# Layer B head loop of a four-layer spectral / recurrent-memory kernel: fixed issue order on three engines, column sums in one block, and PSUM banks shared out anew

## The chip, the cores and the metric

The kernel runs on one core of one Trainium2 chip. The metric is device time in microseconds (us) of the whole launch, lower is better. TensorE is called PE below, VectorE DVE, ScalarE ACT, GpSimd POOL, the DMA-issuing engine SP.

## The reference

Two kinds of layer alternate, A, B, A, B, each after a layer norm and with a residual. The change touches layer B only:

```python
# layer B: S = 2048 tokens of 640 in 64 segments of 32; 8 memory rows; 32 heads of 128
for s in range(n_seg):
    h = concat([mem, xs], axis=1)                      # 40 rows
    q, k, v = h @ Wq, h @ Wk, h @ Wv                   # per head
    p = softmax(where(mask, q @ k.T * Dh**-0.5, -1e9))
    o = (p @ v) @ Wo
    mem = o[:, :M]                                     # goes into the next segment
    outs.append(o[:, M:])
```

The kernel guesses all memories at once, computes all 64 segments in parallel, and checks the guess at the end (a slow path, not taken with these inputs, repeats what fails). So layer B is 32 heads in one long loop, followed by the output projection.

## The kernel before

Work of one head on PE: five Q chains and five K chains (each five accumulating matmuls of up to 502 columns), four or five V tiles, nine score parts (19 matmuls), five value groups (19 matmuls), and the softmax sums: 19 matmuls with a stationary matrix of ones, 128 rows by 32 columns, that write four 32-partition strips of PSUM and so use four column tiles of the array. The heads are staggered: iteration `h` projects head `h`, scores head `h-1` and forms values of head `h-2`. A scheduler decides the final order on each engine.

PSUM has eight banks and before the change all are taken: 2 for projections (`pj`), 2 for scores, 2 for values, 2 for the sums tile `psl`, of whose second bank only 139 columns in one strip are used.

```python
pj = octx.enter_context(tc.tile_pool(name="b_pj", bufs=2, space=PSUM))
pa = octx.enter_context(tc.tile_pool(name="b_pa", bufs=2, space=PSUM))
# ...
def q_run(w, h, g_):
    ps = pj.tile([128, 512], FP32, name="psq", tag="pj")
    chain(w["Wq"], h % 2, ps[:, 0:hi - lo], hT, lo, hi)                    # 5 matmuls
    nc.scalar.mul(out=qv[:, :, 0:SEG], in_=x_view(ps, o, n)[:, :, 1:SW], mul=scale)     # 480 columns
    if g_ < NG - 1:
        nc.vector.tensor_scalar_mul(out=qv[:, :, SEG], in0=..., scalar1=scale)          # 15 columns
    # ... two more small scalings on nc.vector, two on nc.scalar
def k_run(w, h, g_):      # psk in pj, 5 matmuls, one nc.vector copy to KT
def v_tiles(w, hp, t):    # psv in pj, 10 matmuls, one nc.scalar copy to V
def score_part(h, P, part):
    ps = pa.tile([128, 512], FP32, name="pss", tag="pss")
    # ... matmuls K'Q ...
    nc.scalar.activation(out=E[:, 0:n], in_=ps[:, 0:n], func=ACTF.Exp)
    nc.vector.tensor_tensor(out=P[:, o0:o0 + n], in0=E[:, 0:n], in1=bs.mask[:, o0:o0 + n], op=ALU.mult)
def sums(h, P):
    psl = pa.tile([128, 2, 512], FP32, name="psl", tag="psl", bufs=1)
    # ... 19 matmuls with ones32 into psl ...
    nc.scalar.copy(out=sums_sb[:, 0:GQ], in_=psl[:, 0, 0:GQ])
    nc.scalar.copy(out=sums_sb[0:32, GQ:GQ + NL], in_=psl[0:32, 1, 0:NL])
    nc.scalar.activation(out=R[:], in_=sums_sb[:], func=ACTF.Ln, ...)
    nc.scalar.activation(out=R[:], in_=R[:], func=ACTF.Exp, scale=-1.0)    # R = 1 / sums
    # ... R to DRAM, then broadcast to 128 partitions as Rb (1 MB) ...
    nc.gpsimd.tensor_tensor(out=accR[:], in0=accR[:], in1=R[:], op=ALU.add)          # range check
    nc.gpsimd.tensor_tensor(out=accS[:], in0=accS[:], in1=sums_sb[:], op=ALU.add)
# value_group: pso in pa (2 banks); DVE multiplies pso by Rb into oT, oTm
```

## Time and profile before

1843.58 us, median of 3 runs (1839.65 to 1844.62).

Part 1 of the page: busy time of each engine, its share of the span, and instructions.

```profile
span 1841.2 us, 36901 instructions
PE 1709.3 (93%) x14778; PEld 1149.3 (62%) x14779; DVE 938.2 (51%) x2792; ACT 793.7 (43%) x1874; POOL 222.5 (12%) x180
```

A window of the first head loop: its stretch, length, busy time of each engine, granted clock, DMA share and rate.

```profile
core 0: us, PE busy (x) PEld busy (x) DVE busy (x) ACT busy (x) POOL busy (x), PEclk, DMA share, GB/s
303.30:748.00 444.70, 428.28 (x3731) 281.42 (x3727) 253.03 (x776) 245.44 (x611) 76.61 (x50) 1.00 0.36 126
```

PE is busy 96% of the loop and nothing else comes near. "Busy", however, covers matmuls that wait inside their modelled end, so the loop has to be read from the starts of matmuls too. Two heads take 35.5 us (the last sums matmuls of three even heads end at 375.46, 410.96 and 446.46 us). Dividing the start-to-start intervals of PE in four quiet heads (374.9 to 445.95 us) gives, per head, 15.65 us of streaming at N columns / 2.4 + 2.5 ns, 1.08 us around the sums, 0.91 us of waits and 0.11 us of small rest. The Trainium skill, "TensorE: Matmul & The Clock Gate", Back-to-back issue gap, gives that pitch for isolated matmuls on a warm clock, and other figures for a stream in which every matmul has a weight load (about 131 ns at 512 columns, 81 ns at 128). The trace has such a stream (14779 weight loads for 14778 matmuls) and follows the first: the starts are 209 ns apart at 495 columns, 109 ns at 256 and 55 ns at 128.

The waits view of PE: who waited for whom, total us, times, longest.

```profile
PE psq L678 <- DVE QT_2047 L721: 13.7, 15, 1.0
PE psq L678 <- DVE QT_25002 L721: 13.7, 15, 1.0
PE pso L787 <- DVE oTmf L793: 6.9, 11, 1.1
```

The first two lines, one a layer, are Q chains waiting for a projection bank until DVE has done the 15-column scaling. The third is value groups waiting for a value bank, which DVE frees only after it has multiplied by `Rb`: these are the waits for a late broadcast of R, meant by "late broadcast" below. The timelines of PE, DVE and POOL around one such wait (start, duration, engine, line, operation; idle time and its releaser in brackets):

```profile
502.46 1.22 PE L678 MATMUL psq<-hTf,wWq 128*128 128x495 bf16 x5
503.52 0.29 PE L751 MATMUL pss<-QT_2046,KT_2048 128*128 128x132 bf16 x2
504.76 1.21 PE L678 MATMUL psq<-hTf,wWq 128*128 128x499 bf16 x5 [0.96 <-DVE QT_2047 L721]
...
506.33 0.40 PE L787 MATMUL pso<-P,V 128*128 128x132 bf16 x4
506.65 0.23 PE L767 MATMUL psl<-P,ones_72 128*32 128x132 bf16 x1
506.91 0.27 PE L751 MATMUL pss<-QT_2046,KT_2048 128*128 128x141 bf16 x2
507.11 0.23 PE L767 MATMUL psl<-P,ones_72 128*32 128x132 bf16 x1
```

```profile
503.07 1.50 DVE L755 TENSOR_TENSOR P<-E,maskf 128x283 bf16<-128x283 bf16 x1 [0.68 <-ACT E L754]
504.50 0.21 DVE L721 TENSOR_SCALAR QT_2047<-psq 128x15 bf16<-128x15 f32 x1
```

```profile
502.88 1.53 POOL L778 TENSOR_TENSOR accR<-accR,R 128x634 f32<-128x634 f32 x1 [0.45 <-ACT R L772]
```

The mask multiply takes 1.50 us while POOL adds `accR`, the small scaling stands behind it in DVE's queue, and PE stands still for 0.96 us. The PE lines also show the sums (`psl`, tile 128*32) as single matmuls strewn between others; a head has three sums blocks on average.

### The profile page before, as it was taken

The page shows a single profiled execution, that of the slowest core. Times are in us where ns is not written, and L with a number is a line of the kernel's source. Part 1 is how long each engine was busy: PE and PEld are TensorE (multiplying, and loading weights), DVE is VectorE, ACT ScalarE, POOL GpSimd, SP SyncE. Part 2 cuts the span into 40 slices and gives each one's busy share as a digit, 9 for nine tenths or more (in the row PEclk, how much of TensorE's full clock was granted, in tenths as well). Part 3 has the DMA queues.
Part 4 walks back from the last instruction along what each step waited for, and adds up shares of the span by engine and source line. Part 5 has one row for each costly group of instructions (what it writes and reads, how often), then busy time and mean ns, then how long its engine had stood idle before and what let it go on. Part 6 is the DMA issues. An engine that isn't in the chain of part 4 may idle for free. (4 is left out here: it accounts for less than half of the span.)

```text
span 1841.2 us, 36901 instructions
## 1 busy us (share of the span) xinstructions
PE 1709.3 (93%) x14778; PEld 1149.3 (62%) x14779; DVE 938.2 (51%) x2792; ACT 793.7 (43%) x1874; POOL 222.5 (12%) x180
## 2 busy tenths in 40 slices
PE   4987999999999999999959879999999999999998
PEld 2655656666666666677736556666666666666776
DVE  5557255556555555543345562555556555555111
ACT  4334354555555555400023444555555555554000
POOL 0100011111112112100000000111111111111000
PEclk9999999999999999999979989999999999999999
DMA  5764033343343332374164530333433333333630
GB/s 138 190 216 136 16 123 107 121 140 131 104 142 133 118 135 98 129 234 146 51 156 89 217 113 23 117 117 131 146 116 126 128 128 118 134 121 108 208 129 31
DMA packets 148012, 233.10 MB, mean 127 GB/s; under 512 B 8480, under 2 KB 119664, under 8 KB 138096
## 3 DMA queue, kind: packets, MB, share of 16 engines
q1 hardware_dynamic: 141632, 203.72, 32.5%
q0 software_dynamic: 6192, 26.86, 5.8%
q8 instruction: 120, 1.97, 0.4%
q14 instruction: 68, 0.56, 0.1%
HBM read 191.30 MB, written 50.35 MB: 131 GB/s over the span
## 5 line engine op out<-in xcount | busy, mean ns | idle before, releaser
L678 PE MATMUL psq<-hTf,wWq 128*128 128x128 bf16 (+3 forms) x1560 | 310.2, 336 | 36.0 <-DVE QT_2047 L721 13.7
L741 PE MATMUL psv<-wWv,hTf 128*128 128x256 bf16 x2720 | 330.3, 272 | 1.6 <-DVE KT_2048 L734 0.2
L754 ACT ACTIVATE E<-pss 128x269 bf16<-128x269 f32 (+5 forms) x576 | 210.7, 383 | 253.6 <-PE pss L751 240.4
L678 PE MATMUL psk<-hTf,wWk 128*128 128x495 bf16 (+3 forms) x1600 | 317.2, 342 | 0.5 <-DVE hTf L961 0.3
L741 PEld LDWEIGHTS <-hTf 128*128 128x128 bf16 x2720 | 258.0, 97 | 31.4 <-issue 1.7
L755 DVE TENSOR_TENSOR P<-E,maskf 128x269 bf16<-128x269 bf16 (+5 forms) x576 | 221.2, 389 | 65.0 <-ACT E L754 49.7
L743 ACT CAST V<-psv 128x512 bf16<-128x512 f32 (+1 forms) x288 | 162.0, 563 | 207.7 <-PE psv L741 207.7
L678 PEld LDWEIGHTS <-wWq 128*128 128x128 bf16 x1580 | 129.6, 97 | 157.1 <-issue 43.6
L779 POOL TENSOR_TENSOR accS<-accS,sums_sb 128x634 f32<-128x634 f32 x64 | 98.2, 1534 | 998.5 <-ACT sums_sb L770 998.5
L678 PEld LDWEIGHTS <-wWk 128*128 128x128 bf16 x1600 | 136.2, 97 | 113.8 <-issue 1.4
L502 PE MATMUL psx<-Wo_sb,oTxl 128*128 128x320 bf16 x1440 | 203.4, 299 | 0.0
L502 PEld LDWEIGHTS <-oTxl 128*128 128x128 bf16 x1440 | 140.9, 98 | 54.7
L787 PE MATMUL pso<-P,V 128*128 128x132 bf16 (+8 forms) x1216 | 128.5, 216 | 6.9 <-DVE oTmf L793 6.9
L516 DVE TENSOR_TENSOR xo<-psx,xr 128x320 bf16<-128x320 f32 x64 | 31.3, 490 | 175.2 <-PE psx L502 175.2
L791 DVE TENSOR_TENSOR oT<-pso,Rb 128x480 bf16<-128x480 f32 (+1 forms) x160 | 92.9, 581 | 53.3 <-PE pso L787 39.9
L787 PEld LDWEIGHTS <-V 128*128 128x128 bf16 x1216 | 92.7, 98 | 14.5 <-issue 8.2
L778 POOL TENSOR_TENSOR accR<-accR,R 128x634 f32<-128x634 f32 x64 | 97.9, 1529 | 27.4 <-ACT R L772 25.9
L199 PEld LDWEIGHTS <-YT 128*128 128x128 bf16 x640 | 63.1, 99 | 27.1 <-DVE wi L76 2.2
L249 PE MATMUL psg<-GT,UT 128*128 128x320 bf16 x384 | 67.3, 312 | 1.8 <-ACT UT L222 1.8
L89 ACT ACTIVATE lnnb<-lnmv,eps 128x2 f32<-128x2 f32 (+2 forms) x36 | 10.7, 300 | 133.6 <-DVE lnmv L82 132.9
L250 ACT CAST G<-psg 128x640 bf16<-128x640 f32 x64 | 44.3, 692 | 52.4 <-PE psg L249 49.6
L791 DVE TENSOR_TENSOR oT<-pso,oT_2044 128x480 bf16<-128x480 f32 (+1 forms) x80 | 46.5, 581 | 37.1 <-PE pso L787 29.0
(646 smaller groups left out, 2194.6 us busy)
## 6 DMA issues: line engine op xcount, KB each, us to landing
Rb<-Rd SPq DMA_DIRECT2D x32, 1059.5 KB
oTx_d<-oT SPq DMA_DIRECT2D x60, 512.0 KB
oTxl<-oTx_d SPq DMA_DIRECT2D x18, 1024.0 KB
oT_2044<-Rd SPq DMA_DIRECT2D x16, 1059.5 KB
oT_24999<-Rd SPq DMA_DIRECT2D x16, 1059.5 KB
Wv_sb<-in_B_Wv_dram POOLq DMA_DIRECT2D x10, 1024.0 KB, 9.5
wWq<-in_B_Wq_dram SPq DMA_DIRECT2D x32, 320.0 KB
wWk<-in_B_Wk_dram SPq DMA_DIRECT2D x32, 320.0 KB
```

The source lines that it names most:

```text
L199: nc.tensor.matmul(ps[:, cout, 0:NF], lhsT=lhsT, rhs=Fd[:, ch, FD_IDX[(cin, cout)], :], start=(n == 0), stop=(n == 9))
L249: nc.tensor.matmul(psg[:, i, 0:320], lhsT=lhsT, rhs=Gd[:, ch, i * 320:(i + 1) * 320], start=(ch == 0), stop=(ch == 2))
L502: self.tc.nc.tensor.matmul(ps[:, 0:320], lhsT=lhs(h, k // 2 % 4), rhs=self.g["Wo_sb"][:, h, c0:c0 + 320], start=(h == 0), stop=(h == H - 1))
L678: nc.tensor.matmul(ps, lhsT=w[:, ch, hh * 128:(hh + 1) * 128], rhs=src[:, ch, lo:hi], start=(ch == 0), stop=(ch == 4))
L741: nc.tensor.matmul(ps[:, i * 256:(i + 1) * 256], lhsT=hT[:, ch, (t + i) * 128:(t + i + 1) * 128], rhs=w["Wv"][:, ch, :], start=(ch == 0), ...
L743: nc.scalar.copy(out=V[:, t:t + n, :].rearrange("p a b -> p (a b)"), in_=ps[:, 0:n * 256])
L754: nc.scalar.activation(out=E[:, 0:n], in_=ps[:, 0:n], func=ACTF.Exp)
L755: nc.vector.tensor_tensor(out=P[:, o0:o0 + n], in0=E[:, 0:n], in1=bs.mask[:, o0:o0 + n], op=ALU.mult)
L778: nc.gpsimd.tensor_tensor(out=accR[:], in0=accR[:], in1=R[:], op=ALU.add)
L779: nc.gpsimd.tensor_tensor(out=accS[:], in0=accS[:], in1=sums_sb[:], op=ALU.add)
L787: nc.tensor.matmul(pso[:, lo - q0:hi - q0], lhsT=V[:, t, (h % 2) * 128:(h % 2 + 1) * 128], rhs=P[:, off:off + hi - lo], start=(i == 0), st ...
L791: nc.vector.tensor_tensor(out=oT[:, s0 * SEG:(s0 + ns) * SEG].rearrange("p (s t) -> p s t", t=SEG), in0=po[:, :, 0:SEG], in1=pr[:, :, 0:SE ...
```

## The change

Intent: keep PE fed by fixing the issue order of the head loop on PE, ACT and DVE by hand; run the column-tiled sums as one block; put the fifth sums strip into the unused end of the last score bank, so that `psl` needs one bank and projections get three; let ACT alone release a Q bank.

```diff
-    pj = octx.enter_context(tc.tile_pool(name="b_pj", bufs=2, space=PSUM))
+    pj = octx.enter_context(tc.tile_pool(name="b_pj", bufs=3, space=PSUM))
 # q_run, and likewise two more small scalings
-                nc.vector.tensor_scalar_mul(out=qv[:, :, SEG], in0=x_view(ps, o, n)[:, :, 0], scalar1=scale)
+                nc.scalar.mul(out=qv[:, :, SEG], in_=x_view(ps, o, n)[:, :, 0], mul=scale)
 # sums
-            psl = pa.tile([128, 2, 512], FP32, name="psl", tag="psl", bufs=1)
+            psl = pa.tile([128, 512], FP32, name="psl", tag="psl", bufs=1)
+            ps4 = ps_last[0:32, 512 - NL:512]              # end of the last score part's bank
-                    nc.tensor.matmul(psl[32 * j:32 * j + 32, b, ...
+                    dst = psl[32 * g_:32 * g_ + 32, :] if g_ < 4 else ps4
+                    nc.tensor.matmul(dst[:, ...
 # head loop
+        with tc.manual_schedule(engines={nc.tensor.engine, nc.scalar.engine, nc.vector.engine}):
+            for h in range(H + 2):
 # ... dense = Q, K, V pieces; parts = scores; groups = values, interleaved as before ...
+                if h < H:
+                    merge(dense, parts + groups)
+                if 1 <= h <= H:
+                    Rb[h - 1] = sums(h - 1, P[h - 1], last_ps[h - 1])
 # ... the last two iterations and the check's banks rearranged ...
```

The bank count stays at eight: 3 projections, 2 scores, 2 values, 1 sums.

More of the change, by code (lines that the diff above doesn't have):

```diff
@@ L720, in q_run @@
             if g_ < NG - 1:
-                nc.vector.tensor_scalar_mul(out=qv[:, :, SEG], in0=x_view(ps, o, n)[:, :, 0], scalar1=scale)
+                nc.scalar.mul(out=qv[:, :, SEG], in_=x_view(ps, o, n)[:, :, 0], mul=scale)
             if g_ == 0:
-                nc.vector.tensor_scalar_mul(out=QT[:, QPRE:NQ], in0=ps[:, 0:PRE], scalar1=scale)
+                nc.scalar.mul(out=QT[:, QPRE:NQ], in_=ps[:, 0:PRE], mul=scale)
             elif g_ == NG - 2:
@@ L726, in q_run @@
             elif g_ == NG - 1:
-                nc.vector.tensor_scalar_mul(out=x_view(QT, st.qbase(NSEG - 4), 4)[:, :, SEG], in0=ps[:, 0:3 * SW + 1:SW], scalar1=scale)
+                nc.scalar.mul(out=x_view(QT, st.qbase(NSEG - 4), 4)[:, :, SEG], in_=ps[:, 0:3 * SW + 1:SW], mul=scale)
                 q_tail(QT, ps, 0, 3 * SW + 1, SEG - st.TAIL)
@@ L755, in score_part, with sums @@
             nc.vector.tensor_tensor(out=P[:, o0:o0 + n], in0=E[:, 0:n], in1=bs.mask[:, o0:o0 + n], op=ALU.mult)
+            return ps
         runs = [[(t, r) for t in range(NT) for r in st.tiles[t] if r[0] == g_] for g_ in range(NG)]
-        def sums(h, P):
-            psl = pa.tile([128, 2, 512], FP32, name="psl", tag="psl", bufs=1)
+        def sums(h, P, ps_last):
+            psl = pa.tile([128, 512], FP32, name="psl", tag="psl", bufs=1)
+            ps4 = ps_last[0:32, 512 - NL:512]
             for i in range(max(len(r) for r in runs)):
@@ L765, in sums @@
                     t, (_, lo, hi, off) = runs[g_][i]
-                    b, j = divmod(g_, 4)
-                    nc.tensor.matmul(psl[32 * j:32 * j + 32, b, lo - st.q0[g_]:hi - st.q0[g_]], lhsT=ones32[:], rhs=P[:, off:off + hi - lo],
+                    dst = psl[32 * g_:32 * g_ + 32, :] if g_ < 4 else ps4
+                    nc.tensor.matmul(dst[:, lo - st.q0[g_]:hi - st.q0[g_]], lhsT=ones32[:], rhs=P[:, off:off + hi - lo],
                                      start=(i == 0), stop=(i == len(runs[g_]) - 1), skip_group_check=True)
-            nc.scalar.copy(out=sums_sb[:, 0:GQ], in_=psl[:, 0, 0:GQ])
-            nc.scalar.copy(out=sums_sb[0:32, GQ:GQ + NL], in_=psl[0:32, 1, 0:NL])
+            nc.scalar.copy(out=sums_sb[:, 0:GQ], in_=psl[:, 0:GQ])
+            nc.scalar.copy(out=sums_sb[0:32, GQ:GQ + NL], in_=ps4)
             nc.scalar.activation(out=R[:], in_=sums_sb[:], func=ACTF.Ln, bias=g["floor"][:, 0:1])
@@ L815, in begin @@
         def begin():
-            ps = psx()
-            first.append(ps)
-            out.accumulate(ps, len(first) - 1, lambda h, j: oT0[:, h, j * 128:(j + 1) * 128], 0, HPRE)
+            k = len(first)
+            first.append(psx())
+            return [lambda a=a: out.accumulate(first[k], k, lambda h, j: oT0[:, h, j * 128:(j + 1) * 128], a, a + 4) for a in range(0, HPRE, 4)]
         def merge(dense, dep):
@@ L827, in merge @@
                     n += 1
-        P, Rb, oT, w = {}, {}, {}, None
-        for h in range(H + 2):
-            dense, dep = [], []
-            if h < H:
-                if h % 2 == 0:
+        P, Rb, oT, last_ps, w = {}, {}, {}, {}, None
+        with tc.manual_schedule(engines={nc.tensor.engine, nc.scalar.engine, nc.vector.engine}):
+            for h in range(H + 2):
+                if h < H and h % 2 == 0:
                     w = load_w(h // 2)
@@ L842, in _b_fast_pass @@
                     guess[1](pj, vb)
-                if h < 2:
-                    dense.append(lambda: q_m(w, h))
-                else:
-                    dense += [lambda g_=g_: q_run(w, h, g_) for g_ in range(NG)]
-                dense += [lambda g_=g_: k_run(w, h, g_) for g_ in range(NG)]
-                vt = [lambda t=t: v_tiles(w, h // 2, t) for t in range(0, NT, 2)]
-                dense += vt[5:] if h % 2 else vt[:5]
-            else:
-                dense += [begin] * (1 if h == H else 2)
@@ L852, in _b_fast_pass @@
-            if 1 <= h <= H:
-                P[h - 1] = sm.tile([128, st.NP], BF16, name="P", tag="P")
-                dep += [lambda part=part: score_part(h - 1, P[h - 1], part) for part in st.parts]
-            if h >= 2:
-                oT[h - 2] = oTs.tile([128, st.NX], BF16, name="oT", tag="oT")
-                dep += [lambda g_=g_: value_group(h - 2, P[h - 2], Rb[h - 2], oT[h - 2], g_) for g_ in range(NG)]
-            merge(dense, dep)
-            if 1 <= h <= H:
-                Rb[h - 1] = sums(h - 1, P[h - 1])
@@ L861, in _b_fast_pass @@
-            if h >= 2:
-                store(h - 2, oT[h - 2])
+                dense, parts, groups = [], [], []
+                if h < H:
+                    if h < 2:
+                        dense.append(lambda: q_m(w, h))
+                    else:
+                        dense += [lambda g_=g_: q_run(w, h, g_) for g_ in range(NG)]
+                    dense += [lambda g_=g_: k_run(w, h, g_) for g_ in range(NG)]
+                    vt = [lambda t=t: v_tiles(w, h // 2, t) for t in range(0, NT, 2)]
+                    dense += vt[5:] if h % 2 else vt[:5]
@@ new lines, in _b_fast_pass @@
+                if 1 <= h <= H:
+                    P[h - 1] = sm.tile([128, st.NP], BF16, name="P", tag="P")
+                    parts = [lambda part=part: last_ps.update({h - 1: score_part(h - 1, P[h - 1], part)}) for part in st.parts]
+                if h >= 2:
+                    oT[h - 2] = oTs.tile([128, st.NX], BF16, name="oT", tag="oT")
+                    groups = [lambda g_=g_: value_group(h - 2, P[h - 2], Rb[h - 2], oT[h - 2], g_) for g_ in range(NG)]
+                if h < H:
+                    merge(dense, parts + groups)
@@ L864, in _b_fast_pass @@
+                if h == H:
+                    merge(begin(), parts)
+                if 1 <= h <= H:
+                    Rb[h - 1] = sums(h - 1, P[h - 1], last_ps[h - 1])
+                if h == H:
+                    merge(begin(), groups)
+                if h > H:
+                    merge(begin(), [])
+                    merge([lambda: None], groups)
+                if h >= 2:
+                    store(h - 2, oT[h - 2])
     with octx:
@@ L866, in _b_fast_pass @@
         op = octx.enter_context(tc.tile_pool(name="b2_o", bufs=2))
-        psl = pa.tile([128, 2, 512], FP32, name="psl", tag="psl", bufs=1)
-        _b_mem_check(tc, g, pj, [psl[:, 0, :], psl[:, 1, :]], wk, oTm, None,
+        pc = [pa.tile([128, 512], FP32, name="pc0", tag="psl", bufs=1), pa.tile([128, 512], FP32, name="pc1", tag="pso")]
+        _b_mem_check(tc, g, pj, pc, wk, oTm, None,
                      lambda c: [(PRE, st.NC, gq[:, c, 1:NSEG]), (0, PRE, gq[:, c, 1:2].to_broadcast([128, PRE]))], st.NM, st.NC, flag_col,
@@ L885, in psx @@
             n[0] += 1
-            if n[0] % 2:
+            if n[0] % 3:
                 return pj.tile([128, 512], FP32, name="psx", tag="pj")
```

## The prediction

> **What bounds it now.** TensorE. The page of the profile gives PE busy 1709.3 of 1841.2 us (93%), VectorE 51%, ScalarE 43%; the two head loops (220 to 770, 1130 to 1690 us) are 60% of the span. In steady state two heads take 35.5 us there (last sums matmul at 410.86 and 446.36 us in the PE timeline), 17.75 us a head. There PE is 96% busy at granted clock 1.00.
>
> What those 17.75 us hold, from start-to-start intervals of the matmuls in the trace: Q and K chains 8.97 us, V 4.64, scores and values about 1.05 each: 15.7 us of plain streaming. The other 2 us are:
> - Sums. The 128x32 matmuls run 4 to 20 ns apart inside a block, but entering a block delays about 92 ns and leaving it costs 150 to 267 ns. A head has three blocks on average (13 and 6; 12, 5, 1 and 1), about 1.1 us in all. The Trainium skill, "TensorEngine Tiling (Array Packing)", Key Properties, says that changing the tiling mode drains TensorE; the trace agrees.
> - The fourth Q chain waits for a projection bank: the waits view puts 27.4 us, 30 waits, on psq after the VectorE scaling of QT, about 0.96 us every second head. That scaling queues behind a mask multiply that takes 1.50 us instead of 0.3 while GpSimd adds accR. ("GPSIMD Engine Reference", Key points: GpSimd shares SBUF interfaces with VectorE; the trace agrees.) Smaller waits add about 0.3 us a head.
>
> **What the change does.**
> - One sums block per head instead of three: estimate 0.09 + 0.3 + 0.16, so about 0.55 us instead of 1.1. Gain 0.5 us a head.
> - Q banks released by ScalarE alone, three banks instead of two. The small scalings should cost ScalarE about 0.1 us each in its stream (the existing 4- and 28-column ones start the next instruction so soon). Gain about 0.8 us a head.
> - New waits: ScalarE must now finish the four sums instructions (R ready about 2.5 us after the sums) before the first Q scaling. Walking the queue by these durations, third and fifth score part wait for their exponentials: I estimate 0.3 us a head lost.
> - Values stand later as a row (after all scores), so the broadcast of R may bind: the third group needs it about 9.3 us after R is ready. Before, even heads were served by 8.7 and seldom waited; odd heads had the broadcast issued late (4.6 us after R, behind a weight load), and the changed order issues it before that load. I allow 8 us in total for late broadcasts.
> - Tail and output phase stay.
>
> Head: 17.75 to about 16.75 us, 60 heads: 60 us; edge heads 4; minus 8 for late broadcasts. Nearly all is on the critical path: PE is the chain.
>
> **Predicted: 1788 us, range 1770 to 1815.** Faster by over 2%: 0.85, within 2%: 0.14, slower: 0.01.
>
> **What would show it.** Sums: one block of 19 per head, under 0.65 us. Waits view: psq after VectorE QT gone; psq or pss after ScalarE small, under 0.4 us a head. Waits of pso on oTmf still under 15 us. Two heads in 33 to 34 us. PE busy in the loops near 98%. Layer A and output stretches unchanged within 3 us.
>
> **What would make it wrong.** The broadcast of R landing later than 9.3 us in many heads (then about 1815); ScalarE's fixed order holding Q banks longer than walked; small scalings costing 0.2 us each.

## The result, and the profile after

1766.47 us, median of 4 runs (1764.23 to 1768.78). Ratio to before 0.9587, 95% interval 0.9569 to 0.9606: 4.1% faster. The result lies 3.5 us below the predicted range.

Part 1 of the page after, and the window of its first loop:

```profile
span 1762.3 us, 36912 instructions
PE 1664.0 (94%) x14778; PEld 1136.0 (64%) x14779; DVE 863.2 (49%) x2432; ACT 816.8 (46%) x2234; POOL 222.9 (13%) x180
```

```profile
296.00:691.20 395.20, 394.45 (x3581) 265.34 (x3583) 211.96 (x598) 245.38 (x732) 73.66 (x48) 1.00 0.40 136
```

PE is now busy 99.8% of that window. The page's groups of value matmuls, before (first fence) and after (second); the last part of each line is the idle time of PE just before them and its releaser:

```profile
L787 PE MATMUL pso<-P,V 128*128 128x132 bf16 (+8 forms) x1216 | 128.5, 216 | 6.9 <-DVE oTmf L793 6.9
```

```profile
L789 PE MATMUL pso<-P,V 128*128 128x132 bf16 (+8 forms) x1216 | 120.1, 216 | 2.6 <-DVE oTmf L795 2.5
```

The waits that a late broadcast of R causes did not grow but fell, from 6.9 to 2.5 us in these two profiles. The timeline of PE after, from the end of one head to the Q chains of the next:

```profile
492.60 0.27 PE L789 MATMUL pso<-P,V 128*128 128x7 bf16 x3
492.80 0.24 PE L769 MATMUL psl<-P,ones 128*32 128x132 bf16 x4
492.87 0.17 PE L769 MATMUL pss<-P,ones 128*32 128x7 bf16 x1
...
493.26 1.23 PE L678 MATMUL psq<-hTf,wWq 128*128 128x502 bf16 x5
494.33 0.31 PE L751 MATMUL pss<-QT,KT 128*128 128x132 bf16 x3
494.48 1.21 PE L678 MATMUL psq<-hTf,wWq 128*128 128x495 bf16 x5
495.52 0.28 PE L751 MATMUL pss<-QT,KT 128*128 128x148 bf16 x2
495.64 1.21 PE L678 MATMUL psq<-hTf,wWq 128*128 128x495 bf16 x5
496.79 0.28 PE L751 MATMUL pss<-QT,KT 128*128 128x132 bf16 x2
496.91 1.22 PE L678 MATMUL psq<-hTf,wWq 128*128 128x499 bf16 x5
```

All 19 sums matmuls go by between 492.80 and 493.26, and the fourth Q chain (496.91) starts 0.12 us after the score part before it. The timeline of ACT over the same time:

```profile
495.11 0.73 ACT L774 ACTIVATE R<-R 128x634 f32<-128x634 f32 x1
495.75 0.55 ACT L719 ACTIVATE QT<-psq 128x480 bf16<-128x480 f32 x1
496.20 0.23 ACT L721 ACTIVATE QT<-psq 128x15 bf16<-128x15 f32 x1
496.26 0.18 ACT L723 ACTIVATE QT<-psq 128x7 bf16<-128x7 f32 x1
496.32 0.42 ACT L754 ACTIVATE E<-pss 128x283 bf16<-128x283 f32 x1
```

ACT reaches the first Q scaling only at 495.75, 2.5 us after that head's sums, when the third Q chain has already begun in a third bank. With two banks that chain would have needed the first chain's bank, which is read until 496.44.

The same division of PE's starts as before, in four quiet heads (378.6 to 444.5 us), us per head:

| | before | after | prediction took |
|---|---|---|---|
| streaming | 15.65 | 15.65 | 15.7 |
| sums: entering, inside, leaving | 1.08 | 0.55 | 1.1 to 0.55 |
| waits: Q chains before, score parts after | 0.91 | 0.19 | 0.8 to 0.3 |
| small rest | 0.11 | 0.07 | not counted |
| head | 17.75 | 16.46 | 17.75 to 16.75 |

Over 28 heads of each layer the sums' ends advance 499.63 and 498.40 us before, 462.06 and 463.76 us after: 72.2 of the 78.9 us between the two profiled spans. The rest lies outside these heads.

### The profile page after: what moved, and what is told of

Its sections match the earlier page's. It is cut to its first block, busy times and chain, and to the rows that moved or that the text cites. A ratio compares the mean times of both kernels' runs of the same rounds, so it can differ in the third digit from the quotient of the medians.

```text
span 1762.3 us, 36912 instructions
## 1 busy us (share of the span) xinstructions
PE 1664.0 (94%) x14778; PEld 1136.0 (64%) x14779; DVE 863.2 (49%) x2432; ACT 816.8 (46%) x2234; POOL 222.9 (13%) x180
## 5 line engine op out<-in xcount | busy, mean ns | idle before, releaser
L755 DVE TENSOR_TENSOR P<-E,maskf 128x269 bf16<-128x269 bf16 (+5 forms) x576 | 199.6, 355 | 350.1 <-ACT E L754 350.1
L741 PE MATMUL psv<-wWv,hTf 128*128 128x256 bf16 x2720 | 340.4, 272 | 0.0
L754 ACT ACTIVATE E<-pss 128x269 bf16<-128x269 f32 (+5 forms) x576 | 246.3, 429 | 152.0 <-PE pss L751 144.3
L734 DVE CAST KT<-psk 128x495 bf16<-128x495 f32 (+3 forms) x320 | 191.2, 598 | 41.9 <-PE psk L678 41.8
L751 PEld LDWEIGHTS <-KT 128*128 128x128 bf16 x1216 | 113.6, 98 | 116.4 <-issue 16.3
L719 ACT ACTIVATE QT<-psq 128x480 bf16<-128x480 f32 x300 | 170.0, 567 | 0.0
L751 PE MATMUL pss<-QT,KT 128*128 128x132 bf16 (+8 forms) x1216 | 159.5, 216 | 2.7 <-ACT E L754 2.6
L793 DVE TENSOR_TENSOR oT<-pso,oT 128x480 bf16<-128x480 f32 (+1 forms) x160 | 93.2, 583 | 60.3 <-PE pso L789 49.7
L199 PE MATMUL ps<-Fd,YT 128*128 128x321 bf16 x640 | 104.4, 306 | 4.4 <-DMA Fd<-cFd 2.8
L502 PE MATMUL psx<-Wo_sb,oT 128*128 128x320 bf16 x608 | 98.7, 302 | 4.1 <-DVE oT L793 4.1
```

Source lines behind the costliest of these rows:

```text
L199: nc.tensor.matmul(ps[:, cout, 0:NF], lhsT=lhsT, rhs=Fd[:, ch, FD_IDX[(cin, cout)], :], start=(n == 0), stop=(n == 9))
L502: self.tc.nc.tensor.matmul(ps[:, 0:320], lhsT=lhs(h, k // 2 % 4), rhs=self.g["Wo_sb"][:, h, c0:c0 + 320], start=(h == 0), stop=(h == H - 1))
L734: nc.vector.tensor_copy(out=KTs[h % 2][:, lo:hi], in_=ps[:, 0:hi - lo])
L741: nc.tensor.matmul(ps[:, i * 256:(i + 1) * 256], lhsT=hT[:, ch, (t + i) * 128:(t + i + 1) * 128], rhs=w["Wv"][:, ch, :], start=(ch == 0), ...
L751: nc.tensor.matmul(ps[:, off - o0:off - o0 + hi - lo], lhsT=KT[:, t * 128:(t + 1) * 128], rhs=QT[:, lo:hi], start=True, stop=True)
L793: nc.vector.tensor_tensor(out=oT[:, s0 * SEG:(s0 + ns) * SEG].rearrange("p (s t) -> p s t", t=SEG), in0=po[:, :, 0:SEG], in1=pr[:, :, 0:SE ...
```

## The experiments

Each ran three timed rounds against the kernel before, and each gave a correct result. "Per head" is the advance of the sums' ends over 24 heads of the first layer; the ledgers are those of the table, over the same 24 heads, so that they hold occasional waits for late broadcasts too (before: 17.89 us a head, waits 1.06; after: 16.49 us, waits 0.23). A run with another number of projection banks also shares the tiles of the output phase (`psx`) out over the banks accordingly; the diffs leave that line out.

### Scalings on ACT alone

```diff
 # kernel before, q_run: three small scalings
-  nc.vector.tensor_scalar_mul(...)
+  nc.scalar.mul(...)
```

> Kernel before, with only the small Q scalings moved from VectorE to ScalarE. Theory A (the Q chain waits because the VectorE scaling queues behind a slow mask multiply): the waits of psq on VectorE QT, 27 us in total before, vanish and most of the 0.9 us of waits a head goes, so 1800 to 1812 us. Theory B (two banks or the scheduled order hold PE, whoever does the scaling): the wait only changes its name to ScalarE, and the time stays within 8 us of 1843. The sums blocks stay at about three a head in both.

Measured 1849.11 us, ratio 1.0045 (1.0023 to 1.0067): slightly slower, within 2%. Theory A fails here. The 27.4 us of Q waits on DVE are gone; a smaller Q wait on ACT and other waits stand in their place, as the waits view of PE shows:

```profile
PE psv L741 <- DVE KT L734: 13.5, 16, 1.9
PE psq L678 <- ACT QT L723: 11.9, 58, 0.5
PE pss L751 <- ACT E L754: 10.6, 28, 0.4
```

The ledger has 0.89 us of waits a head and 1.35 us for the sums, which the scheduler now puts into 3.5 blocks. Taking DVE out of the release of a bank brought nothing here, with two banks; since the scheduler also rearranged the sums, this run does not show what the move does with the order held.

### No additions on POOL

```diff
-            nc.gpsimd.tensor_tensor(out=accR[:], in0=accR[:], in1=R[:], op=ALU.add)
-            nc.gpsimd.tensor_tensor(out=accS[:], in0=accS[:], in1=sums_sb[:], op=ALU.add)
```

> Kernel before without the two GpSimd additions per head (they only feed a range check, which then always passes; the output stays right). If the slow mask multiply is made by GpSimd on the shared memory interface, the 283-column multiply falls from a mean of 862 ns to about 300, the psq waits on VectorE QT fall from 27 us to under 5, and the time falls by 20 to 35 us. If the multiply is slow for another reason, or the wait has another cause, neither moves: within 8 us of 1843.

Measured 1807.49 us, ratio 0.9819 (0.9797 to 0.9840): 34 us less. The group of the 283-column mask multiply, before and in this run (busy us, mean ns, idle before):

```profile
L755 DVE TENSOR_TENSOR P<-E,maskf 128x283 bf16<-128x283 bf16 x64 | 55.2, 862 | 20.2 <-ACT E L754 20.2
```

```profile
L755 DVE TENSOR_TENSOR P<-E,maskf 128x283 bf16<-128x283 bf16 x64 | 19.5, 305 | 20.1 <-ACT E L754 20.1
```

The waits of `psq` on DVE's scaling, 27.4 us before, no longer stand in this run's waits view, and PE runs its matmuls of the loop in the same order as before. So the prediction's origin of the wait is shown: POOL's additions stretch the mask multiply and with it the wait for the Q bank. The Trainium skill says in "GPSIMD Engine Reference", Key points, that POOL shares its SBUF interfaces with VectorE and contends with two-input instructions; 862 against 305 ns agrees. In the trace before, all 60 mask multiplies of over 0.6 us overlap an addition on POOL and end 0.15 to 0.17 us after it. But this kernel cannot drop the additions, which feed the range check. This is a diagnosis, not a version.

### The fixed order alone

```diff
 # changed kernel, with
-  pj bufs=3, psl one bank, small scalings on nc.scalar
+  pj bufs=2, psl two banks, small scalings on nc.vector
```

> The fixed order alone, with its one sums block per head, but two projection banks, a two-bank sums tile, and the Q scalings on VectorE as before. Theory A: the sums blocks give 0.54 us a head (32 us), but ScalarE now finishes the four sums instructions before the first Q scaling, so with two banks the third Q chain waits about 0.9 us in every head, and the wait behind the mask multiply stays: 1835 to 1875 us. Theory B (the fixed order is what brings the gain): under 1790.

Measured 1886.28 us, ratio 1.0239 (1.0220 to 1.0258): 45 us slower than before. The sums are in one block (0.55 us a head), yet a head takes 18.45 us. The waits view of PE:

```profile
PE psq L678 <- ACT E L754: 50.1, 60, 0.8
PE psk L678 <- ACT QT L685: 36.8, 60, 0.6
PE psv L741 <- DVE KT L734: 12.7, 63, 0.5
```

The ledger has 2.19 us of waits a head. Fixing this order with two banks stalls Q, K and V chains in every head: ACT comes to the Q banks only after the four sums instructions, and PE, in strict order, has nothing to fill in.

### The changed kernel under the scheduler

```diff
-        with tc.manual_schedule(engines={nc.tensor.engine, nc.scalar.engine, nc.vector.engine}):
+        with ExitStack():
```

> The changed kernel with the three engines' fixed order taken off: the scheduler decides again; three banks and scalings on ScalarE stay. If the gains add: the Q waits stay gone (about 0.7 us a head) and the sums lie in about three blocks again (0.54 us a head lost): 1795 to 1810. If the order makes the whole gain: above 1825. If the order is worth nothing: within 8 us of 1766.

Measured 1764.23 us, ratio 0.9578 (0.9560 to 0.9596), against 0.9587 of the changed kernel: the same. The expected 1795 to 1810 was a miss. In the loop the scheduler itself puts the 19 sums matmuls into one block a head; over 24 heads its order of PE's 3588 matmuls is the fixed one. So the fixed order is worth nothing here, and the single block does not come from it.

### Scalings back on DVE

```diff
 # changed kernel, q_run: three small scalings
-  nc.scalar.mul(...)
+  nc.vector.tensor_scalar_mul(...)
```

> The changed kernel with the small Q scalings back on VectorE; order and three banks stay. Theory A (the move to ScalarE removes the wait): the fourth and fifth Q chain wait again behind the mask multiply, 1790 to 1810. Theory B (the third bank hides it): walking the queues, the slow multiply ends about 0.3 us before the bank is needed, so within 8 us of 1766.

Measured 1759.05 us, ratio 0.9555 (0.9534 to 0.9576): within the band of theory B, and 7 us below the changed kernel by the medians, though the intervals overlap. In the ledger the score waits of 0.19 us a head are gone and 0.05 us of waits remain. So in the fixed order that wait is made by the small scalings in ACT's queue. Whether the move costs time is not shown: under the scheduler the kernel with three banks is no faster with them on DVE (1767.67 us, "The third bank alone") than on ACT (1764.23 us, the run above).

### Two projection banks

```diff
-    pj = octx.enter_context(tc.tile_pool(name="b_pj", bufs=3, space=PSUM))
+    pj = octx.enter_context(tc.tile_pool(name="b_pj", bufs=2, space=PSUM))
```

> The changed kernel with two projection banks; order and ScalarE scalings stay. ScalarE starts the first Q scaling 2.4 us after the sums, so the third Q chain, due 2.4 us after the sums, waits until about 3.2: 0.8 us a head, 1805 to 1825. If the third bank is not needed once the scalings are on ScalarE: within 8 us of 1766.

Measured 1853.07 us, ratio 1.0057 (1.0040 to 1.0073): the whole gain is lost, 87 us, more than expected, although PE's order in the loop is that of the changed kernel. The waits view of the first loop (285 to 715 us, 24 heads):

```profile
PE psq L678 <- ACT QT L723: 16.6, 24, 0.7
PE psk L678 <- ACT QT L685: 6.9, 24, 0.3
PE psv L741 <- DVE KT L734: 4.2, 22, 0.2
```

The expected wait of the third Q chain is there, 0.69 us on average in this view and 0.86 us by starts; the first K chain (0.46) and the first V tile (0.36) also wait, which the expectation had not counted.

### Three sums blocks, first try

```diff
+   step = [lambda i=i: sum_steps(h - 1, P[h - 1], last_ps[h - 1], i, i + 1) for i in range(2)]
+   groups = groups[:2] + step[:1] + groups[2:4] + step[1:] + groups[4:]
    merge(dense, parts + groups)
```

> The changed kernel with the 19 sums matmuls of a head in three blocks (two pieces of five and four go between value groups), nothing else moved. If entering and leaving a block is the cost: two more blocks of about 0.09 plus 0.15 us a head, 60 heads: 25 to 35 us slower than 1766. If the cost is the matmuls themselves: within 8 us of 1766.

Measured 1841.65 us, ratio 0.9993 (0.9977 to 1.0010): 75 us slower than the changed kernel, far over the expectation. The experiment was not clean. Two more pieces in the merge list shifted the interleaving, so that two score parts followed the first Q chain and the third part came too early. Its timeline of PE:

```profile
498.69 0.38 PE L678 MATMUL psq<-hTf,wWq 128*128 128x502 bf16 x1
498.90 0.43 PE L751 MATMUL pss<-QT,KT 128*128 128x132 bf16 x5
499.16 1.21 PE L678 MATMUL psq<-hTf,wWq 128*128 128x495 bf16 x5
501.37 0.28 PE L751 MATMUL pss<-QT,KT 128*128 128x132 bf16 x2 [1.00 <-ACT E L754]
```

Of the loss, 0.36 us a head (0.91 against 0.55) lies around the sums; 1.16 us is this new wait. What follows about blocks is nothing yet; about fixed orders, that one score part moved forward can cost a microsecond in every head.

### Three sums blocks in place

```diff
-   groups = groups[:2] + step[:1] + groups[2:4] + step[1:] + groups[4:]
+   groups[1] = lambda a=groups[1], b=step[0]: (a(), b())
+   groups[3] = lambda a=groups[3], b=step[1]: (a(), b())
```

> The changed kernel with the sums in three blocks, each early piece now tied to the value group ahead of it, so that no score part moves. If a block's entering and leaving is the cost: 0.36 us a head by the trace of the first try, 22 us, so 1784 to 1794 us, and no wait of a score part over 0.3 us. If it is free: within 8 us of 1766. If the 75 us of the first try were all due to the blocks: above 1825.

Measured 1790.52 us, ratio 0.9706 (0.9688 to 0.9724): 24 us slower than the changed kernel. The sums take 0.91 us a head instead of 0.55, and the score waits 0.25 us instead of 0.19. So a further block costs 0.18 us, and two of them in 60 heads an estimated 22 us (60 x 0.36); the profiled run, 30 us slower, had more late broadcasts too. The Trainium skill, "TensorEngine Tiling (Array Packing)", Key Properties, says that changing the tiling mode drains TensorE. The trace agrees with a cost at each change, and its size is now known for this loop.

### The third bank alone

```diff
 # kernel before, scheduler order, scalings on nc.vector
-    pj ... bufs=2
+    pj ... bufs=3
-            psl = pa.tile([128, 2, 512], ...)
+            psl = pa.tile([128, 512], ...)
+            ps4 = ps_last[0:32, 512 - NL:512]
```

> The kernel before with the third projection bank and the one-bank sums tile that frees it, nothing else: the scheduler orders, VectorE scales. Theory now: the third bank takes the Q wait out of PE's way and, because the scheduler then sees no gap to fill, leaves the sums in one block. So it makes the whole gain: 1752 to 1768 us, at or below the changed kernel, PE waits under 0.25 us a head. Rival: fixed order or ScalarE scalings have a part of their own: 1785 or more.

Measured 1767.67 us, ratio 0.9590 (0.9574 to 0.9606): the whole gain, with no fixed order and no scaling moved. Its PE order in the steady loop is that of the changed kernel, sums block included. The Q wait on DVE, 27.4 us before, has shrunk to this line of the waits view:

```profile
PE psq L678 <- DVE QT L721: 0.4, 2, 0.2
```

The ledger has 0.55 us for the sums and 0.42 us of waits a head, of which 0.20 are late broadcasts (five in 24 heads of this run); without them the waits are 0.22, of which, by starts, 0.14 are Q chains and 0.08 score parts.

### The one-bank sums tile alone

```diff
 # as the last one, but
-    pj ... bufs=3
+    pj ... bufs=2
```

> As the run with the third bank alone, but with two projection banks: the one-bank sums tile by itself. If the bank makes the gain, the Q wait is back (about 0.9 us a head) and the built order shows two sums blocks a head (one saved, 0.28 us): 1820 to 1848 us. If the tile itself were the gain: under 1790.

Measured 1834.32 us, ratio 0.9953 (0.9936 to 0.9969). The Q wait is back in the waits view of PE:

```profile
PE psq L678 <- DVE QT L721: 29.2, 31, 1.0
```

There are two sums blocks a head (0.78 us). Between this run and the one before, 67 us, lies only the third bank. By the two ledgers it takes 0.80 us a head off the waits (1.22 to 0.42) and 0.23 us off the sums, which the scheduler then puts into one block.

### The sums block early, fixed order

```diff
                 if h < H:
+                    if groups:
+                        groups.insert(1, lambda: Rb.update({h - 1: sums(h - 1, P[h - 1], last_ps[h - 1])}))
                     merge(dense, parts + groups)
-                if 1 <= h <= H:
+                if h == 1 or h == H:
                     Rb[h - 1] = sums(h - 1, P[h - 1], last_ps[h - 1])
```

> The changed kernel with the sums block one value group after the last score part, before most V tiles, instead of at the head's end. ScalarE then does the sums instructions in the V phase and the broadcast of R has 5 us more. Expected: the two score waits (0.19 us a head, 11 us) and the late-broadcast waits (about 4 us in all) go: 1748 to 1758 us. Rival: the four sums instructions hold up the V evictions on ScalarE, PE waits for V banks instead: 1762 to 1785.

Measured 1739.41 us, ratio 0.9444 (0.9429 to 0.9460): 27 us below the changed kernel, more than expected. It is the best version here. The window of its first loop:

```profile
273.00:663.00 390.00, 390.00 (x3570) 264.36 (x3569) 200.97 (x599) 249.97 (x732) 73.67 (x48) 1.00 0.45 139
```

PE is never idle. The ledger has no wait over 40 ns in 24 heads, late broadcasts included, and both layers take 16.27 us a head. The early place also moves POOL's additions away from the mask multiplies: 62 of these last over 0.6 us in the changed kernel's trace, 2 in this one. What that brings was not tested; in the changed kernel with the scalings on DVE, 62 such multiplies left PE no score wait in the ledger of its first layer. The rival, that V evictions would be held up on ACT, is refuted. The size was missed because the expectation counted 15 us of waits at once, whereas the profiled span fell by 24.1 us: 28 heads of a layer gain about 0.23 to 0.30 us each by the head periods (16.50 and 16.56 to 16.27), 15 us in both layers. The remaining 9 us lie outside the steady heads and were not taken apart.

### The sums block early, scheduler order

```diff
 # the version above, with
-        with tc.manual_schedule(...):
+        with ExitStack():
```

> The version with the early sums block, with the fixed order taken off. In its built order the sums stay one block, early. If the fixed order is worth nothing here either: within 8 us of 1739. If the early place needs it: 1750 or more.

Measured 1744.63 us, ratio 0.9466 (0.9450 to 0.9482). The steady head is 16.27 us, without waits, as in the fixed order. Of the 4.0 us between the two profiled spans, 3.6 lie outside the stretches between the first and the last sums of each layer, and the intervals overlap. The early place, not the fixed order, brings the gain.

## Why the prediction was right or wrong

Direction, the chain (PE), the size of the sums and the unchanged stages were right. The time was too high by 21.5 us and fell outside the range.

- **Sums: right.** "One sums block per head instead of three: ... about 0.55 us instead of 1.1." Measured 0.55 and 1.08. The run with three blocks in place confirms it from the other side: 0.36 us a head for two more blocks.
- **The failing step: the waits.** "Gain about 0.8 us a head", "I estimate 0.3 us a head lost" and "I allow 8 us in total for late broadcasts" make 0.5 us a head less 8 us. In quiet heads the waits fell from 0.91 to 0.19, that is 0.72 (0.73 unrounded). Both terms were mis-sized: all 0.91 us of waits before went instead of 0.8 (by starts the fourth Q chain lost 1.13 us every second head, not the 0.96 us of the waits view), and the new score waits cost 0.19 instead of 0.3. The late-broadcast waits fell too, by 4.4 us (6.9 to 2.5 in one profile each; other runs with three banks and one sums block had 2.9 to 9.1), instead of costing 8. For the 56 heads counted above, the prediction comes to 56 x 1.0 - 8 = 48 us and the trace to 72.2; the edges gave 6.7 us where, in the same count, 8 were expected. So the miss lies in the loop. The broadcast allowance was wrong in kind: such waits stood in the kernel before as well, and the changed order starts to issue the broadcast of odd heads about 1.9 us after R instead of 4.1 (the prediction's 4.6). Only a difference should have been booked.
- **The credit was wrong.** The prediction gave the waits to "Q banks released by ScalarE alone, three banks instead of two" together. The moved scalings alone made the kernel before 0.45% slower; the third bank alone made the whole gain (ratio 0.9590 against 0.9587). With the third bank and the fixed order, the 0.19 us of score waits a head come and go with the scalings on ACT; that leaving them on DVE is faster (1759.05 against 1766.47 us) is not shown, for the intervals overlap and under the scheduler the two places differ the other way (1767.67 and 1764.23 us).
- **The order was not the lever.** The prediction booked the single block to the change as a whole, and the change's intent booked it to the fixed order. With three banks the scheduler builds the same block by itself; with two it builds two to three and a half blocks a head. That it strews sums into gaps which it foresees while a bank is missing is inferred from the built orders, not shown.
- **The origin of the wait: right.** Without POOL's additions the mask multiply is 305 instead of 862 ns and the time 34 us less. The third bank does not remove this slow multiply (in the changed kernel the group's mean is 917 ns); it takes it off PE's path.

Open: what the early sums block gains outside the steady heads, and whether it gains further with the scalings on DVE, which was not run (no wait is left in its loop to remove).

## What to carry to other kernels

When PE waits for a PSUM bank, count which use holds each of the eight banks and for how long, before reordering anything: here 139 columns held a whole bank, and moving them into the unused end of another freed the one bank that was worth 4%. "Perfetto Trace Analysis", Matmul Optimizations, of the Trainium skill advises to use all eight banks; both kernels do, and what counted was who had them. Then look for a place in the iteration where a serial stretch on another engine (here 2.5 us of sums instructions on ACT) meets slack instead of the busiest bank traffic: that gave another 1.5%. And test each part of a bundled change alone: here the bank made the gain, the fixed order did nothing with three banks, and the moved scalings brought no clear gain anywhere.

## What the Trainium skill lacked or had wrong

- "TensorEngine Tiling (Array Packing)" states the drain on a change of tiling mode but gives no size. Here entering a 128x32 block delays about 92 ns, the first matmul after one starts 0.10 to 0.27 us after the block's last, and two more blocks cost 0.36 us a head.
- "TensorE: Matmul & The Clock Gate": of its two accounts of the pitch, the one for a stream with weight loads does not hold here. The starts lie 209 ns apart at 495 columns and 55 ns at 128, as its formula for isolated matmuls has it.
- "ScalarE: Activation LUTs", What ACT_TABLE_LOAD costs, says that back-to-back ACTIVATEs overlap by about 93 ns. Here that holds behind longer ones (0.09 us behind 634 columns, 0.10 behind 480), but ones of 15 and 7 columns, 0.23 and 0.18 us long, let the next start after 0.06 us, an overlap of 0.17 and 0.12 us; they cost ACT a third of their duration or less.
- No page weighs one use of a PSUM bank against another. Here both kernels take all eight, and a third projection bank was worth 67 us with the scheduler and 87 us with a fixed order; it replaced a sums bank that was nearly empty.
